# Attention, greedy MoE and Sinkhorn MoE in one kernel: GpSimd taken out of the routing rounds, and each expert's tokens turned inside the second layer of the expert ahead

## The chip, the cores and the metric

The kernel runs on one core of one Trainium2 chip. The metric is the device time of one execution in microseconds; the median of several runs counts. TensorE is called PE below, VectorE DVE, ScalarE ACT, GpSimd POOL; SP is the engine whose queue issues most DMAs.

## What is computed

Three stages follow each other, all in float32. Attention with a sink of 4 keys and a window of 128 over 2 x 8 heads, 768 positions, 64 dimensions gives 1536 tokens of 512 values. A first mixture of experts routes greedily: all 1536 x 8 logits are walked through from the highest down, a token goes to the first expert that still has room for it (192 tokens each), and only that expert's two layers run on it. A second mixture runs all 8 experts on every token and weighs them with a matrix P that eight Sinkhorn steps normalise by rows and columns.

```python
for idx in order:
    tok, e = (int(idx) // E, int(idx) % E)
    if assigned[tok] >= 0 or counts[e] >= cap:
        continue
    assigned[tok] = e
    counts[e] += 1
...
    h = np.maximum(x[mask] @ w1[e], 0.0)
    out[mask] = h @ w2[e]
...
    h = np.maximum(x @ w1[e], 0.0)
    ye = h @ w2[e]
    out += P[:, e:e + 1] * ye
```

## The kernel before

**Routing.** The greedy walk is done in eight rounds (`route`, L580). Each round fills one expert: every token proposes its best open expert, and `count` (L549) finds for each token how many proposals of the same expert stand ahead of it. For that, DVE builds for every chunk `c` of 128 tokens a 0/1 block `g` (which tokens have a higher logit, L566 and L568) and the block on the diagonal, `gt`, where equal logits count only if they come earlier. For odd chunks `gt` is one DVE operation (L561), for even ones two POOL operations (L564, L565). PE multiplies the blocks with the proposals into `cnt` (L574). There are twelve chunks in rounds 1 to 3, then `compact` (L493) squeezes the open tokens into six chunks for rounds 4 to 7; round 0 uses counts made during attention. From `cnt` DVE and PE find the expert that is full first, its tokens' slots as one-hot blocks `oh` (L623), their indices `ix` (L637), and `gather` (L658) has POOL issue two indirect DMAs that fetch the expert's 192 tokens into `xg` (two tiles, one buffer each). Weights of the expert come in four 1 MB DMAs on SP's queue (`load_w`, L647).

**First MoE.** `moe1(r)` (L689) turns the gathered tokens by eight PE transposes (L699) and two ACT copies (L701) into `xe` (one buffer), runs the first layer (L707, copied by ACT to `hT`, L709), then the second (L718, two halves of two blocks each, copied by ACT to `yT`, L720). `operands(r)` (L668) then splits results, and for experts 2, 3, 6 and 7 four sums `T1` to `T4` of results (DVE, L679 to L682), into a rounded part (ACT, L686) and a low part, the rest (L687: POOL, for the last expert DVE). The second MoE multiplies with these. Last come the logits of the second MoE (L727). All the PSUM tiles of the expert work are called `mm` and share three buffers. For expert 0 an edge (`issue_after`) keeps the transposes behind the third group of counts of round 1.

**Order.** The loop at L732 traces round `r` with high priority and then `moe1(r - 1)`; a planner at build time gives every engine one fixed order, routing first where it takes it to be ready, expert work in between. After the loop come the preparation of the first weights of the second MoE (`prepare`, L432: ACT rounds them, POOL makes sums `S` and the low parts, L447 to L452 and L464) and `moe1(7)`. On the chip each engine issues its own list in order.

**Second MoE.** `moe2` (L755) is a long pipeline of matmuls (L800, L857) over 32 chunks of weights, from about 430 us to the end.

Of the kernel before, what the change touches and what calls it, by code (L numbers as in the profile page):

```python
# [8 lines left out]
F32 = mybir.dt.float32  # L9
# [4 lines left out]
OP = mybir.AluOpType  # L14
# [6 lines left out]
def kernel(  # L21
# [16 lines left out]
    nc = tc.nc  # L38
    B, H, S, D = q.shape
    N, DM = out.shape  # L40
    E = moe_w_gate.shape[1]
    F = moe_w1.shape[2]
    P = 128
# [3 lines left out]
    CAP = N // E  # L47
# [15 lines left out]
    KD = DM // P  # L63
# [28 lines left out]
    before = rp.tile([P, P], F32, name="before")  # L92
# [3 lines left out]
    beforeb = rp.tile([P, P], BF, name="beforeb")  # L96
# [374 lines left out]
    def routing_and_moe1():  # L471
# [3 lines left out]
        mp = cx.enter_context(tc.tile_pool(name="mp", bufs=2))  # L475
# [10 lines left out]
        nc.gpsimd.tensor_copy(mv[:, :, 4 * E:], code)  # L486

        IDX = {}
        TP = 2
        st = dict(n=NCH, L=L, val=val, code=code, prop=prop0, m=m0)  # L490
        BIG = 2.0 ** 100

# [56 lines left out]
        def count(n, m, prop, row):  # L549

            cnt = ps.tile([P, n, E], F32, name="cnt", bufs=1)
            nc.tensor.matmul(cnt.rearrange("p c e -> p (c e)"), zb, zb[:, :n * E], start=True, stop=False,
                             skip_group_check=True)
            for c0 in range(0, n, GC):
                c1 = min(n, c0 + GC)
                blocks = []
                for c in range(c0, c1):
                    g = gp.tile([P, n, P], BF, name="g", bufs=GB)
                    gt = gp.tile([P, P], BF, name="gt", bufs=GB)
                    if c % TP:  # L560
                        nc.vector.scalar_tensor_tensor(gt, row[:, c], m[:, c:c + 1], before, op0=OP.is_equal,  # L561
                                                       op1=OP.mult)
                    else:
                        nc.gpsimd.tensor_scalar(gt, row[:, c], m[:, c:c + 1], None, op0=OP.is_equal)  # L564
                        nc.gpsimd.tensor_mul(gt, gt, beforeb)  # L565
                    nc.vector.tensor_scalar(g[:, :c + 1], row[:, :c + 1], m[:, c:c + 1], None, op0=OP.is_lt)  # L566
                    if c + 1 < n:
                        nc.vector.tensor_scalar(g[:, c + 1:], row[:, c + 1:], m[:, c:c + 1], None, op0=OP.is_le)  # L568
                    blocks += [(c, gt, prop[:, c, :])] + [(cc, g[:, cc, :], prop[:, c, :]) for cc in range(n)]

                first = None
                for cc, a, b in reversed(blocks):
                    with nullcontext() if first is None else tc.issue_after(first.ins):
                        mm = nc.tensor.matmul(cnt[:, cc, :], a, b, start=False, stop=(a is blocks[0][1] and c1 == n),  # L574
                                              skip_group_check=True)
                    first = first or mm
                st.setdefault("counted", []).append(mm.ins)
            return cnt
# [62 lines left out]
        W, XG, YT = {}, {}, {}  # L641
# [5 lines left out]
        def load_w(r, mats=(0, 1), q=nc.sync):  # L647
            e = q.value_load(EIX[0:1, r:r + 1], min_val=0, max_val=E - 1)
            for a in mats:
                src = (moe_w1, moe_w2)[a][bass.ds(e, 1)].rearrange("o (k p) f -> p (o k) f", p=P)  # L650
                for h in range(2):
                    t = bp.tile([P, WT], F32, name="wf", tag="w", bufs=WB)
                    t = t.rearrange("p (k f) -> p k f", f=DM if a else F // 2)
                    q.dma_start(t, src[:, h * KF // 2:(h + 1) * KF // 2] if a
                                else src[:, :, h * F // 2:(h + 1) * F // 2])
                    W.setdefault(r, ([], []))[a].append(t)
# [11 lines left out]
        def operands(r):  # L668
            t, h = divmod(r, 4)
            h, o = divmod(h, 2)  # L670
            K2_ = KD // 2
            block = lambda r: (YT[r // 2][:, a * K2_:(a + 1) * K2_, r % 2 * CAP:(r % 2 + 1) * CAP] for a in (0, 1))
            lo, hi = block(r)
            if h == 0:
                new = {"B11": lo, "B21": hi}
            else:
                lo0, hi0 = block(r - 2)
                T = {n: mp.tile([P, K2_, CAP], F32, name=n, bufs=1) for n in ("T1", "T2", "T3", "T4")}
                nc.vector.tensor_sub(T["T1"], lo, lo0)  # L679
                nc.vector.tensor_sub(T["T2"], hi, T["T1"])  # L680
                nc.vector.tensor_sub(T["T3"], hi, lo)
                nc.vector.tensor_sub(T["T4"], hi0, T["T2"])  # L682
                new = {"B22": hi, **T}
            for n, x in new.items():
                xh, xl = (y[:, :, o * CAP:(o + 1) * CAP] for y in XO[n][t])
                nc.scalar.activation(xh, x, AF.Copy)  # L686
                (nc.vector if r == E - 1 else nc.gpsimd).tensor_sub(xl, x, xh.bitcast(F32))  # L687

        def moe1(r):  # L689

            w1, w2 = W.pop(r)
            xg = XG.pop(r)
            xe = mp.tile([P, KD, CAP], F32, name="xe", bufs=1)
            with tc.issue_after(st["counted"][KC]) if r == 0 else nullcontext():
                for k0 in range(0, KD, 2):
                    pt = pm.tile([P, 2, CAP], F32, name="mm", tag="mm", bufs=3)
                    for k in (k0, k0 + 1):
                        for a in range(2):
                            nc.tensor.transpose(pt[:, k - k0, a * HC:(a + 1) * HC], xg[a][:HC, k * P:(k + 1) * P],  # L699
                                                ident[:HC, :HC])  # L700
                    nc.scalar.activation(xe[:, k0:k0 + 2, :], pt, AF.Copy)  # L701
            hT = mp.tile([P, KF, CAP], F32, name="hT", bufs=1)
            for j0 in range(0, KF, 2):
                ph = pm.tile([P, 2, CAP], F32, name="mm", tag="mm", bufs=3)
                for j in (j0, j0 + 1):
                    for k in range(KD):
                        nc.tensor.matmul(ph[:, j - j0, :], w1[j // JH][:, k, j % JH * P:(j % JH + 1) * P], xe[:, k, :],  # L707
                                         start=(k == 0), stop=(k == KD - 1))
                nc.scalar.activation(hT[:, j0:j0 + 2, :], ph, AF.Relu)  # L709
            if r % 2 == 0:  # L710
                YT[r // 2] = mp.tile([P, KD, 2 * CAP], F32, name="yT", bufs=2)
            yT = YT[r // 2]
            s0 = r % 2 * CAP
            for k0 in range(0, KD, 2):
                py = pm.tile([P, 2, CAP], F32, name="mm", tag="mm", bufs=3)
                for k in (k0, k0 + 1):
                    for j in range(KF):
                        nc.tensor.matmul(py[:, k - k0, :], w2[j // JH][:, j % JH, k * P:(k + 1) * P], hT[:, j, :],  # L718
                                         start=(j == 0), stop=(j == KF - 1))
                nc.scalar.activation(yT[:, k0:k0 + 2, s0:s0 + CAP], py, AF.Copy)  # L720
            operands(r)

            c0, c1 = s0 // P, (s0 + CAP) // P
            pl = ps.tile([P, 2, E], F32, name="lg", bufs=1)
            for a in range(c0, c1):
                for k in range(KD):
                    nc.tensor.matmul(pl[:, a - c0, :], yT[:, k, a * P:(a + 1) * P], wg2[:, k, :],  # L727
                                     start=(k == 0), stop=(k == KD - 1))
            c = r // 2 * (2 * CAP // P)
            nc.vector.tensor_copy(L2[:, c + c0:c + c1, :], pl[:, :c1 - c0, :])  # L730

        for r in range(E):  # L732
            with tc.high_priority(offset=HP):
                got = route(r)
                place_tokens(r, *got)
                if r + 1 == E // 2:
                    compact(NC2)
                if r + 1 < E:
                    propose()
                if r == 0:  # L740

                    with tc.issue_after(st["shown"]):
                        load_w(0, (1,), nc.scalar)
            if r == E - 1:
                rcx.close()
                pools.append(ctx.enter_context(tc.tile_pool(name="stg", bufs=1, side="right", reuse_waits="tile")))
            if r > 0:
                moe1(r - 1)
        run(prepare(*chunks[0]))
        moe1(E - 1)  # L750
        return cx

    def moe2(cx):  # L755
# [127 lines left out]
        for n in range(len(units) + 1):  # L883
# [7 lines left out]
            for _ in range(7):  # L891
# [4 lines left out]
                next(b, None)  # L896

    cx = routing_and_moe1()
    cx.close()
    moe2(ctx)  # L900
# [33 lines left out]
```

## Time and profile before

| what | value |
|---|---|
| median of 3 runs | 1449.2 us (1447.0 to 1450.65) |
| the profiled execution, its own time | 1455.11 us |
| its span, first to last instruction | 1453.0 us |
| its mean granted PE clock | 0.973 |
| PE busy | 1403.7 us, 97% of the span |
| DVE, ACT, POOL busy | 833.8, 461.8, 487.7 us |

The profile is one execution, recorded instruction by instruction. Busy times say how long an engine had something to do; what an engine waited for is put down to the instruction that released it. The granted clock of PE has two levels, 2.4 GHz (1.0) and 1.2 GHz (0.5); a value in between is the mean over a stretch.

### The profile page before, as it was taken

Reading aid. Unit: us, or ns where it says so; the run is one execution under the profiler, and the core shown is the slowest. Engines: PE = TensorE matmul, PEld = TensorE weight load, DVE = VectorE, ACT = ScalarE, POOL = GpSimd, SP = SyncE. Lnnn points to the kernel's source line nnn. Section 1 sums busy time; section 2 is a strip of 40 time slices with the busy share of each in tenths; the row PEclk is TensorE's granted clock in tenths of the full one; section 3 lists DMA queues with packets and bytes.
Section 4 is the critical chain, followed back from the end, with each engine's and each line's share of the span. In section 5 each row is a group of like instructions: output and inputs, shape, how many; then the busy total and the mean of one; then the engine's idle time right before and its main releaser. Section 6 shows DMA issues by size and latency. Waiting matters only on the chain.

```text
span 1453.0 us, 20938 instructions
## 1 busy us (share of the span) xinstructions
PE 1403.7 (97%) x8275; PEld 1241.0 (85%) x8275; DVE 833.8 (57%) x1822; ACT 461.8 (32%) x975; POOL 487.7 (34%) x472
## 2 busy tenths in 40 slices
PE   7999599999988999999999999999999999999998
PEld 4667499889987889888889889889888888888987
DVE  4667777771037565555555555555655555555554
ACT  4566111121233333223223223323323323323321
POOL 1136554351262223223433223433322432322303
PEclk9999599999998999999999999999999999999999
DMA  7331445657611000100100100100100100100002
GB/s 128 95 78 38 123 147 128 178 84 203 215 44 30 29 30 29 44 29 29 44 30 30 44 30 30 44 30 30 44 29 29 44 30 30 39 34 30 15 1 87
DMA packets 87338, 87.39 MB, mean 60 GB/s; under 512 B 43976, under 2 KB 60360, under 8 KB 87240
## 3 DMA queue, kind: packets, MB, share of 16 engines
q1 hardware_dynamic: 82696, 74.50, 17.9%
q0 software_dynamic: 2944, 9.44, 2.8%
q10 hardware_dynamic: 1600, 2.11, 0.4%
q8 instruction: 65, 1.06, 0.3%
q14 instruction: 33, 0.27, 0.1%
HBM read 79.75 MB, written 6.30 MB: 59 GB/s over the span
## 4 chain that ended last, share of the span: by engine, by line
PE 88%; DVE 7%; issue 1%; DMA 1%; ACT 1%; POOL 1%; SPq 0%; POOLq 0%; DVEq 0%; ACTq 0%
PE pa L857 36%; PE X L800 18%; PE Z L800 9%; PE mm L707 6%; PE Y L800 5%; PE mm L718 3%; PE S L241 2%; PE o L296 2%; PE PT L283 2%; DVE g L568 1%; PE ms L308 1%; DMA wf<-in_moe_w_dram 1%; DVE g L566 1%; PE tr L217 1%; PE cnt L574 1%
## 5 line engine op out<-in xcount | busy, mean ns | idle before, releaser
L857 PE MATMUL pa<-w,h 128*128 128x512 f32 x2304 | 597.2, 395 | 0.0
L857 PEld LDWEIGHTS pa<-w,h 128*128 128x128 f32 x2304 | 427.8, 188 | 67.8 <-ACT h L807 0.3
L868 DVE SCALAR_TENSOR_TENSOR accs<-pa,Pm,accs 128x512 f32<-128x512 f32 x360 | 269.1, 748 | 211.9 <-PE pa L857 211.9
L808 DVE SCALAR_TENSOR_TENSOR h<-sum,h 128x384 fp32r<-128x384 f32 x192 | 156.1, 813 | 99.1 <-ACT h L807 99.0
L447 POOL TENSOR_TENSOR w1l<-r,w1h 128x512 fp32r<-128x512 f32 x64 | 64.7, 1032 | 429.8 <-ACT w1h L446 416.3
L807 ACT ACTIVATE h<-sum 128x384 fp32r<-128x384 f32 x192 | 100.4, 523 | 207.9 <-DVE sum L817 207.9
L464 POOL TENSOR_TENSOR w<-r,w 128x1024 fp32r<-128x1024 f32 x32 | 77.0, 2407 | 235.6 <-ACT w L463 235.6
L812 ACT ACTIVATE u<-X 128x384 f32<-128x384 f32 x64 | 31.5, 492 | 268.6 <-PE X L800 268.6
L707 PE MATMUL mm<-xe,wf 128*128 128x192 f32 x512 | 104.6, 360 | 3.6 <-ACT xe L701 3.6
L707 PEld LDWEIGHTS mm<-xe,wf 128*128 128x128 f32 x512 | 92.3, 210 | 5.4 <-ACT xe L701 4.3
L718 PE MATMUL mm<-hT,wf 128*128 128x192 f32 x512 | 90.2, 329 | 0.0
L447 POOL TENSOR_TENSOR w1l<-S,w1h 128x1024 fp32r<-128x1024 f32 x32 | 86.9, 2714 | 0.0
L718 PEld LDWEIGHTS mm<-hT,wf 128*128 128x128 f32 x512 | 82.9, 190 | 0.0
L817 DVE TENSOR_TENSOR sum<-Z,u 128x384 f32<-128x384 f32 x64 | 35.7, 558 | 58.9 <-ACT u L812 58.9
L812 ACT ACTIVATE v<-X 128x384 f32<-128x384 f32 x64 | 31.4, 491 | 78.0 <-PE X L800 78.0
L254 ACT ACTIVATE pb<-pb,nb 128x264 f32<-128x264 f32 (+1 forms) x96 | 46.5, 488 | 14.4 <-DVE nb L249 13.2
L808 DVE SCALAR_TENSOR_TENSOR h<-X,h 128x384 fp32r<-128x384 f32 x64 | 35.7, 558 | 22.0 <-ACT h L807 22.0
L817 DVE TENSOR_TENSOR sum<-Z,v 128x384 f32<-128x384 f32 x64 | 35.7, 558 | 18.6 <-PE Z L800 18.5
L807 ACT ACTIVATE h<-X 128x384 fp32r<-128x384 f32 x64 | 31.5, 492 | 46.2 <-PE X L800 46.1
L446 ACT ACTIVATE w1h<-r 128x512 fp32r<-128x512 f32 x64 | 30.0, 516 | 48.5 <-PE Z L800 46.2
L244 DVE CUSTOM_DVE_ANT_0 pb<-S,M 128x264 f32<-128x264 f32 (+1 forms) x96 | 36.5, 403 | 13.9 <-PE S L241 13.1
L709 ACT ACTIVATE hT<-mm 128x384 f32<-128x384 f32 x32 | 15.7, 490 | 88.2 <-PE mm L707 83.8
(291 smaller groups left out, 2435.2 us busy)
## 6 DMA issues: line engine op xcount, KB each, us to landing
r<-in_moe_w_dram SPq DMA_DIRECT2D x64, 512.0 KB, 3.5
wf<-in_moe_w_dram SPq DMA_DIRECT2D x30, 1024.0 KB, 7.1
kn<-in_k_dram SPq DMA_DIRECT2D x12, 256.0 KB, 3.7
qn<-in_q_dram SPq DMA_DIRECT2D x12, 256.0 KB, 3.9
vn<-in_v_dram SPq DMA_DIRECT2D x12, 256.0 KB, 3.7
X<-xs POOLq DMA_DIRECT2D x12, 256.0 KB, 2.4
wf<-in_moe_w_dram ACTq DMA_DIRECT2D x2, 1024.0 KB, 11.4
xg<-X,ix POOLq DMA_INDIRECT x16, 8.7
```

The source lines that it names most:

```text
L254: nc.scalar.activation(PB[c][:, h, :w], PB[c][:, h, :w], AF.Exp, bias=NB[c][:, 0, h:h + 1], scale=scale, accum_out=NB[c][:, 2, h:h + 1])
L447: nc.gpsimd.tensor_sub(w1[1][:, o:o + n], x, w1[0][:, o:o + n].bitcast(F32))
L464: nc.gpsimd.tensor_sub(w2[:, 1], r2, w2[:, 0].bitcast(F32))
L707: nc.tensor.matmul(ph[:, j - j0, :], w1[j // JH][:, k, j % JH * P:(j % JH + 1) * P], xe[:, k, :], start=(k == 0), stop=(k == KD - 1))
L718: nc.tensor.matmul(py[:, k - k0, :], w2[j // JH][:, j % JH, k * P:(k + 1) * P], hT[:, j, :], start=(j == 0), stop=(j == KF - 1))
L800: nc.tensor.matmul(acc_, w1[a][:, o, k, :], XO[x][t][b][:, k, :], start=(start and n == 0), stop=(stop and n == 3 * KH - 1), skip_group_ch ...
L807: nc.scalar.activation(t[:, 0], x, AF.Relu)
L808: nc.vector.scalar_tensor_tensor(t[:, 1], x, 0.0, t[:, 0].bitcast(F32), op0=OP.max, op1=OP.subtract)
L812: nc.scalar.activation(t, x, AF.Copy)
L817: nc.vector.tensor_add(t, a, b)
L857: nc.tensor.matmul(pa, HT[u, f, h][:, a, j * P:(j + 1) * P], w2[:, b, f, :], start=(n == 0), stop=(n == 3 * FP - 1))
L868: nc.vector.scalar_tensor_tensor(acc[:, c], pa, pe, acc[:, c], op0=OP.mult, op1=OP.add)
```

## The change

Three edits. The diagonal blocks `gt` are all built by DVE, in one operation each; the two POOL operations for even chunks go. The low parts in `operands` are all subtracted by DVE. And the turning of the tokens becomes a function of its own, `turn_tokens(r)`: it is called within the second layer of expert `r - 1`, after the first half of that layer is copied to `yT`, and for expert 0 directly ahead of `moe1(0)`, where it stood before.

```diff
--- before.py
+++ after.py
@@ -486,7 +486,6 @@
         nc.gpsimd.tensor_copy(mv[:, :, 4 * E:], code)
 
         IDX = {}
-        TP = 2
         st = dict(n=NCH, L=L, val=val, code=code, prop=prop0, m=m0)
         BIG = 2.0 ** 100
 
@@ -557,12 +556,7 @@
                 for c in range(c0, c1):
                     g = gp.tile([P, n, P], BF, name="g", bufs=GB)
                     gt = gp.tile([P, P], BF, name="gt", bufs=GB)
-                    if c % TP:
-                        nc.vector.scalar_tensor_tensor(gt, row[:, c], m[:, c:c + 1], before, op0=OP.is_equal,
-                                                       op1=OP.mult)
-                    else:
-                        nc.gpsimd.tensor_scalar(gt, row[:, c], m[:, c:c + 1], None, op0=OP.is_equal)
-                        nc.gpsimd.tensor_mul(gt, gt, beforeb)
+                    nc.vector.scalar_tensor_tensor(gt, row[:, c], m[:, c:c + 1], before, op0=OP.is_equal, op1=OP.mult)
                     nc.vector.tensor_scalar(g[:, :c + 1], row[:, :c + 1], m[:, c:c + 1], None, op0=OP.is_lt)
                     if c + 1 < n:
                         nc.vector.tensor_scalar(g[:, c + 1:], row[:, c + 1:], m[:, c:c + 1], None, op0=OP.is_le)
@@ -684,13 +678,14 @@
             for n, x in new.items():
                 xh, xl = (y[:, :, o * CAP:(o + 1) * CAP] for y in XO[n][t])
                 nc.scalar.activation(xh, x, AF.Copy)
-                (nc.vector if r == E - 1 else nc.gpsimd).tensor_sub(xl, x, xh.bitcast(F32))
-
-        def moe1(r):
-
-            w1, w2 = W.pop(r)
+                nc.vector.tensor_sub(xl, x, xh.bitcast(F32))
+
+        XE = {}
+
+        def turn_tokens(r):
+
             xg = XG.pop(r)
-            xe = mp.tile([P, KD, CAP], F32, name="xe", bufs=1)
+            xe = XE[r] = mp.tile([P, KD, CAP], F32, name="xe", bufs=1)
             with tc.issue_after(st["counted"][KC]) if r == 0 else nullcontext():
                 for k0 in range(0, KD, 2):
                     pt = pm.tile([P, 2, CAP], F32, name="mm", tag="mm", bufs=3)
@@ -699,6 +694,12 @@
                             nc.tensor.transpose(pt[:, k - k0, a * HC:(a + 1) * HC], xg[a][:HC, k * P:(k + 1) * P],
                                                 ident[:HC, :HC])
                     nc.scalar.activation(xe[:, k0:k0 + 2, :], pt, AF.Copy)
+
+        def moe1(r):
+
+
+            w1, w2 = W.pop(r)
+            xe = XE.pop(r)
             hT = mp.tile([P, KF, CAP], F32, name="hT", bufs=1)
             for j0 in range(0, KF, 2):
                 ph = pm.tile([P, 2, CAP], F32, name="mm", tag="mm", bufs=3)
@@ -718,6 +719,8 @@
                         nc.tensor.matmul(py[:, k - k0, :], w2[j // JH][:, j % JH, k * P:(k + 1) * P], hT[:, j, :],
                                          start=(j == 0), stop=(j == KF - 1))
                 nc.scalar.activation(yT[:, k0:k0 + 2, s0:s0 + CAP], py, AF.Copy)
+                if k0 == 0 and r + 1 < E:
+                    turn_tokens(r + 1)
             operands(r)
 
             c0, c1 = s0 // P, (s0 + CAP) // P
@@ -744,6 +747,8 @@
             if r == E - 1:
                 rcx.close()
                 pools.append(ctx.enter_context(tc.tile_pool(name="stg", bufs=1, side="right", reuse_waits="tile")))
+            if r == 1:
+                turn_tokens(0)
             if r > 0:
                 moe1(r - 1)
         run(prepare(*chunks[0]))
```

## Rows read from the trace of the kernel before

**Rows 1.** The page: busy time of each engine, share of the span, instructions.
```profile
PE 1403.7 (97%) x8275; PEld 1241.0 (85%) x8275; DVE 833.8 (57%) x1822; ACT 461.8 (32%) x975; POOL 487.7 (34%) x472
```

**Rows 2.** Busy time by stretch; last three: granted PE clock, DMA share, GB/s.
```profile
190.00:340.00 150.00, 141.96 (x1336) 130.63 (x1333) 110.26 (x358) 30.05 (x61) 66.03 (x72) 0.94 0.58 147
480.00:1453.00 973.00, 966.70 (x4817) 867.93 (x4815) 558.26 (x816) 298.45 (x551) 306.19 (x241) 1.00 0.10 34
```

**Rows 3.** Timeline of PE: start, us, engine, line, tiles, [idle before <-releaser].
```profile
204.45 0.18 PE L574 MATMUL cnt<-prop,gt 128*128 128x8 bf16 x1 [0.65 <-POOL gt L565]
...
293.98 0.18 PE L574 MATMUL cnt<-prop,gt 128*128 128x8 bf16 x1 [1.82 <-POOL gt L565]
...
332.85 1.12 PE L628 MATMUL sm<-oh,codec 128*2 128x192 bf16 x6 [2.43 <-DVE oh L623]
...
405.30 12.19 PE L707 MATMUL mm<-xe,wf 128*128 128x192 f32 x56 [3.37 <-ACT xe L701]
```

**Rows 4.** Busy time by stretch, where the granted clock is low.
```profile
216.70:222.20 5.50, 5.49 (x40) 5.32 (x41) 1.12 (x4) 0.34 (x1) 0.70 (x1) 0.50 0.00 0
293.98:297.00 3.02, 3.02 (x13) 3.02 (x14) 2.51 (x6) 0.52 (x1) 1.86 (x2) 0.67 0.20 23
297.00:300.00 3.00, 3.00 (x17) 3.00 (x17) 1.90 (x14) 0.49 (x1) 1.00 (x1) 0.76 0.10 8
333.00:336.00 3.00, 3.00 (x14) 2.14 (x12) 0.35 (x1) 0.49 (x1) 0.00 (x0) 0.50 0.42 124
336.00:340.00 4.00, 4.00 (x16) 3.98 (x17) 0.16 (x1) 0.00 (x0) 0.00 (x0) 0.58 0.74 262
405.00:408.00 3.00, 2.70 (x8) 2.70 (x9) 0.00 (x0) 0.25 (x1) 3.00 (x4) 0.50 0.00 0
408.00:412.00 4.00, 4.00 (x17) 4.00 (x17) 0.00 (x0) 0.49 (x1) 2.76 (x4) 0.62 0.00 0
```

**Rows 5.** Groups by line, 160 to 428 us, and one DVE instruction of the timeline.
```profile
L564 POOL TENSOR_SCALAR gt<-row,m 128x128 bf16<-128x128 f32 x30 | 31.8, 1064 | 21.8 <-DVE ix L637 10.6 <-ACT row L546 8.4 <-PE cnt L574 2.5
L565 POOL TENSOR_TENSOR gt<-gt,beforeb 128x128 bf16<-128x128 bf16 x30 | 19.4, 653 | 1.6
...
L561 DVE SCALAR_TENSOR_TENSOR gt<-row,m,before 128x128 bf16<-128x128 f32 x30 | 12.3, 410 | 0.0
...
424.46 0.56 DVE L687 TENSOR_TENSOR xT1l<-T,xT1h 128x384 fp32r<-128x384 f32 x1 [0.59 <-ACT xT1h L686]
```

**Rows 6.** Timeline of DVE and POOL in round 7.
```profile
327.43 2.88 DVE L606 TENSOR_SCALAR eh<-iota_e,t 128x8 f32<-128x8 f32 x1
...
327.36 1.01 POOL L687 TENSOR_TENSOR xT2l<-T,xT2h 128x384 fp32r<-128x384 f32 x1
...
329.27 1.01 POOL L687 TENSOR_TENSOR xT4l<-T,xT4h 128x384 fp32r<-128x384 f32 x1
```

**Rows 7.** Timeline of POOL, DVE and ACT between the last two experts.
```profile
401.24 2.65 POOL L447 TENSOR_TENSOR w1l<-S,w1h 128x1024 fp32r<-128x1024 f32 x1
...
401.62 2.69 DVE L682 TENSOR_TENSOR T<-yT,T 128x384 f32<-128x384 f32 x1
...
404.34 0.52 ACT L686 ACTIVATE xT4h<-T 128x384 fp32r<-128x384 f32 x1 [2.09 <-DVE T L682]
404.77 0.47 ACT L701 ACTIVATE xe<-mm 128x384 f32<-128x384 f32 x1
```

**Rows 8.** POOL's gathers and ACT's copy, timeline; DMA issues: count, us to landing.
```profile
199.75 0.99 POOL L663 DMA_INDIRECT xg<-X,ix  x1 [13.06 <-DVE ix L637]
...
202.44 1.37 POOL L663 DMA_INDIRECT xg<-X,ix  x1 [0.17 <-issue]
...
207.13 0.49 ACT L720 ACTIVATE yT<-mm 128x384 f32<-128x384 f32 x1 [5.98 <-PE mm L718]
...
xg<-X,ix POOLq DMA_INDIRECT x16, 8.7
...
xg<-X,ix POOLq DMA_INDIRECT x1, 13.4
```

## The prediction

> **What bounds the kernel now.** I read the page first: TensorE (PE) is busy 1403.7 us of a span of 1453.0 [rows 1], so only what it waits, or runs at a lower clock, can be saved. The table by stage says where not to look: from 480 us to the end it is busy 966.7 of 973 us at full clock, and no edit is in that stage [rows 2]. From 190 to 340 us, where rounds of routing and the first MoE share the engines, it waits some 8 us and its granted clock is 0.94 [rows 2]. PE's timeline with the releasers of its waits gives the ones that bear on the change [rows 3]: 0.65 us at 204 for a `gt` of GpSimd (POOL), and a second just like it in the next round; 1.82 us at 294 for another; 2.43 us at 333 for a one-hot `oh` of VectorE (DVE); 3.37 us at 405 for the tokens `xe` of the last expert. The longer ones cost twice. Behind them the granted clock falls from 2.4 to 1.2 GHz: in the windows of [rows 4] the share lost is one minus the clock, so 3.0 us at 0.67 and 3.0 at 0.76 lose 1.0 + 0.7 = 1.7 us after the wait at 294; 1.5 + 1.7 = 3.2 after 333; 1.5 + 1.5 = 3.0 after 405. Behind the 0.65 us no fall is seen; I count none there.
>
> **Diagonals (L560 to L565).** Thirty pairs on POOL go, 31.8 + 19.4 us of its time [rows 5], and DVE gets thirty `gt` of the kind of L561, mean 0.41 us: 12.3 us over seven rounds, 2.5 in each of three rounds with twelve chunks, 1.2 in each of four with six. DVE gets something back: some of its time is waiting for POOL. The plainest case is in round 7: L606, an operation on 128x8, lasts 2.88 us, and it ends with the last of three subtractions of POOL that fill 327.4 to 330.3 [rows 6]. What POOL's diagonals hold in this way no row isolates. Bounds: nothing comes back (2.5 us a long round, 12.3 in all), or all that POOL did in the pairs (51.2 us [rows 5]) had stood in DVE's way, more than DVE gets. I take an even trade, near the lower end, because most `gt` of POOL are short beside a long `g`; then the rounds keep their length, and PE, which has expert work to fill in, sees nothing of it. What it does see is that the two waits of 0.65 and that of 1.82 on POOL go, since there is no `gt` left behind POOL's gathers: 3.1 us, and 1.7 of clock. **Gain 4.8.** What is late next is DVE's own `g`, on which PE already waits here and there.
>
> **Low parts (L687).** 23 subtractions for experts 0 to 6 go from POOL to DVE at 0.56 us each, the length of the one that DVE makes already [rows 5]: 12.9 us, two for each of experts 0, 1, 4 and 5, five for 2, 3 and 6. POOL's three at 327.4 were what held L606, and with it the chain to `oh`, on which PE waited 2.43 us. Without them the 2.88 us go; up to three subtractions, 1.7 us, may come between the links of the same chain, which leaves 2.88 - 1.7 = 1.2 and PE a wait of 2.43 - 1.2 = 1.2; at best the wait is gone. I keep 0.6 us of wait and let the clock stand: **gain** 2.43 - 0.6 + 3.2 = **5.0**, with 1.2 (half of the wait gone, the clock falling all the same) and 5.6 as ends. A low part waits for ACT's copy `xh`; behind it on DVE queue the next links of routing, which are due first in the planner's order, so I cost that at nothing while ACT is idle for most of the stage (30 of 150 us busy [rows 2]).
>
> **Turning the tokens ahead.** Eight transposes and two copies per expert move from behind the logits of the expert ahead into the middle of its second layer. The count of instructions stays; no DMA moves. For the last expert the gain is plain: its second copy to `xe` stood on ACT at 404.77, directly behind `xT4h`, which waited 2.09 us for the `T4` of DVE, which in turn lasted 2.69 beside a 2.65 us subtraction of POOL [rows 7]. Turned half a layer earlier, these copies come ahead of all of that: the wait of 3.37 and 3.0 us of clock go, **gain 6.4**. `T4` stays late, but nothing of PE waits for it in the next layer: the copies to `hT` come behind it on ACT, and three PSUM buffers cover them. If that cover were gone, the 2.09 us of ACT's wait would come back.
>
> Each gather into the single buffers `xg` is released earlier too, which is good for experts 5 to 7. For expert 1 it turns against the change. Its turn was due after expert 0; now it stands at the copy of the first half of `yT`, 207.13 before [rows 8], 206.5 without the wait at 204. Its second gather was issued at 202.44 behind a `gt`; without it, it follows the first one directly, 199.75 + 0.99, say 200.8 [rows 8]. Landing takes 8.7 us in the median of sixteen [rows 8], so 209.5: PE, which issues in order, would stand 3.0 us in the middle of the layer. Nothing in the trace shows this wait; its ends are none (the planner puts other work ahead) and the longest landing, 13.4 us [rows 8], that is 214.2 - 206.5 = 7.7 us. I take the median. For the clock I take 1.7, the loss behind the 1.82 us wait, between nothing behind 0.65 and 3.2 behind 2.43. **Loss 4.7.** The Trainium skill (SBUF — State Buffer, section "SBUF: two separate sides") warns of just this: descriptors of a DMA issued by GpSimd are held up while VectorE runs operations in a two-port mode. By that rule the 13.4 would be the figure to use, since DVE computes `g` without a break in that stretch, and the sum would lose 10.9 here, not 4.7; that landing is a rival below.
>
> **Sum.** 4.8 + 5.0 + 6.4 - 4.7 = 11.5 us off. The profiled execution took 1455.1 us by its own time, 5.9 above the median of the runs; I take the difference over to the median: 1449.2 - 11.5 = 1437.7.
>
> **Rivals.** (1) The gather lands late. For it: gathers run beside busy DVE, and one took 13.4. Against: expert 1's first one is of the ordinary kind. The stand is 7.7 us and the clock loses 3.2, 10.9 in place of 4.7: 1443.9. (2) DVE becomes the bound of the rounds, and the kernel gets slower. Nothing of POOL's absence comes back, each long round is 2.5 us longer by six `gt`, later ones also by low parts; expert 1's gather is issued 2.5 us later against a PE that isn't, so 3.0 + 2.5 + 3.2 = 8.7 us are lost at its turn, at most the same at expert 2's, and the wait for `oh` at 333 stays: 4.8 + 6.4 - 17.4, that is 6.2 slower, 1455.4. It decides once DVE gets back less than about half of what it is given. Against it speaks the 2.88 us L606 [rows 6]: what POOL does is felt on DVE. (3) The planner doesn't turn early: it holds the transposes back behind the rest of the layer. Then there is neither the gain of 6.4 nor the loss of 4.7: 9.8 off, 1439.4. (4) Better than the forecast: no stand at expert 1, the whole of 5.6 at 333, and the slow stretch from 216.7 to 222.2 at 0.50 [rows 4], 2.8 us lost behind a thin stretch of small matmuls that the transposes leave, goes as well: 4.8 + 5.6 + 6.4 + 2.8 = 19.6, 1429.6.
>
> **Chances.** Forecast 0.50, rival 1 0.17, rival 2 0.11, rival 3 0.13, rival 4 0.09. Runs of this kernel differ by a few us, so 0.3% (4.3 us) is about the least that a measurement tells from no change. Rival 2 is slower. Rival 1 lies at the edge of it, so a part of it counts as the same, with a part of the forecast's upper end: faster 0.79, same 0.11, slower 0.10. The range goes from rival 4 to just past rival 1, 1429 to 1445; it leaves out rival 2 and the tails.
>
> **What would show it.** Right: no wait of PE on POOL between 190 and 340 us; L606 of round 7 at the length of its neighbours; PE going from the last second layer but one into the last expert without a gap, its clock at 1.0 there; a wait of some 3 us at expert 1's turn, with the gather's landing at its end. Wrong: a longer DVE stretch from the first to the last `g` of a round (rival 2), transposes still behind the logits (rival 3), or a wait at expert 1 over 5 us (rival 1). Falls of the clock at new places would break the sum even with each step right.

## The result, and the profile after

| | kernel before | changed kernel |
|---|---|---|
| median, first measurement | 1449.93 us (4 runs) | 1434.58 us (1433.8 to 1440.94, 4 runs) |
| ratio, 95% interval | | 0.9904 (0.9882 to 0.9927) |
| the same kernel once more, last experiment below | 1449.95 us (11 runs) | 1436.12 us (6 runs), 0.9907 (0.9879 to 0.9935) |
| the profiled execution: own time, span | 1455.11, 1453.0 us | 1440.94, 1439.2 us |

So 14 to 15 us are gone; 11.5 were forecast, and 1434.6 to 1436.1 lies 2 to 3 us under the 1437.7, inside the range. The ratios, here and below, are as they were measured; they differ by up to 0.2% from the quotient of the medians beside them. In the page POOL lost 76 us of work, DVE got 5 more in total, PE is busy 9 us less with the same 8275 instructions [rows 1]:

```profile
PE 1394.8 (97%) x8275; PEld 1233.9 (86%) x8275; DVE 839.0 (58%) x1875; ACT 460.9 (32%) x975; POOL 412.0 (29%) x389
```

Where the time went is seen best from the end of attention to the first matmul of the Sinkhorn step, 438.84 us before and 425.39 after. The stretches by table, first the kernel before, then the changed one (columns as in [rows 2]):

```profile
160.00:438.00 278.00, 252.86 (x2118) 238.00 (x2117) 147.78 (x432) 59.31 (x118) 117.07 (x119) 0.91 0.55 145
```
```profile
160.00:424.60 264.60, 244.20 (x2118) 231.31 (x2117) 153.27 (x485) 58.48 (x118) 41.63 (x36) 0.94 0.57 152
190.00:340.00 150.00, 145.65 (x1405) 136.18 (x1403) 109.05 (x395) 30.87 (x63) 10.50 (x10) 0.97 0.56 148
340.00:415.00 75.00, 75.00 (x483) 74.62 (x483) 13.30 (x20) 21.29 (x44) 19.78 (x18) 1.00 0.60 172
```

Both traces are of executions 5 to 6 us above the median of their kernel, so they can be compared. PE has the same 2118 matmul records in both, in 13.4 us less. Of these, 4.7 are waits (278.00 - 252.86 = 25.1 before, 264.60 - 244.20 = 20.4 after), and 8.7 are busy time, because less of the same work ran at 1.2 GHz: the granted clock is 0.94 in place of 0.91. From 340 to 415 us, where the kernel before stood 3.37 us for the last expert's tokens, PE is never idle and its clock is 1.0. Not all is gain: from 318 to 322 us the clock of the changed kernel was 0.58, some 1.7 us lost, with PE busy all that time and no wait ahead of it.

The waits that [rows 3] list are all gone; there are new ones, on the gathers. PE's timeline after (columns as in [rows 3]; `mm<-ident,xg` is the turning of tokens: the first row is expert 0, the next two expert 1, the fourth expert 2; the last is the first matmul of the Sinkhorn step), and a row of the table by stretch:

```profile
181.00 1.38 PE L694 MATMUL mm<-ident,xg 96*128 96x96 f32 x7 [1.40 <-DMA xg<-X,ix]
...
208.00 0.30 PE L694 MATMUL mm<-ident,xg 96*128 96x96 f32 x1 [1.65 <-DMA xg<-X,ix]
210.14 1.22 PE L694 MATMUL mm<-ident,xg 96*128 96x96 f32 x6 [1.84 <-DMA xg<-X,ix]
...
245.09 0.80 PE L694 MATMUL mm<-ident,xg 96*128 96x96 f32 x7 [0.86 <-DMA xg<-X,ix]
...
425.39 0.48 PE L770 MATMUL gmx<-ident,gm 128*128 128x128 f32 x1 [3.73 <-DVE gm L768]
...
209.40:216.20 6.80, 6.06 (x46) 6.05 (x47) 2.73 (x6) 1.39 (x3) 0.00 (x0) 0.50 0.02 5
```

Expert 1's turn costs 1.65 + 1.84 = 3.5 us of waiting, and from 209.4 us, within the second wait, to 216.2 the clock is down (0.50): PE is busy for 6.06 us of that, so 3.0 are lost. DVE's operations of the rounds, by groups, 160 to 428 us, first before, then after (L600 is the former L606):

```profile
L566 DVE TENSOR_SCALAR g<-row,m 128x128 bf16<-128x128 f32 (+11 forms) x60 | 37.4, 633 | 2.8 <-ACT row L546 2.6
L568 DVE TENSOR_SCALAR g<-row,m 128x640 bf16<-128x640 f32 (+10 forms) x53 | 32.3, 618 | 0.1
L606 DVE TENSOR_SCALAR eh<-iota_e,t 128x8 f32<-128x8 f32 x8 | 5.2, 654 | 0.3
```
```profile
L560 DVE TENSOR_SCALAR g<-row,m 128x128 bf16<-128x128 f32 (+11 forms) x60 | 34.0, 566 | 0.0
L562 DVE TENSOR_SCALAR g<-row,m 128x640 bf16<-128x640 f32 (+10 forms) x53 | 28.2, 539 | 0.1
L559 DVE SCALAR_TENSOR_TENSOR gt<-row,m,before 128x128 bf16<-128x128 f32 x60 | 20.7, 344 | 10.2 <-PE cnt L568 7.6 <-ACT row L545 2.7
L600 DVE TENSOR_SCALAR eh<-iota_e,t 128x8 f32<-128x8 f32 x8 | 1.8, 230 | 0.2
```

Sixty `gt` cost 20.7 us where thirty cost 12.3 [rows 5], 8.4 more; the blocks `g` give back 3.4 + 4.1 = 7.5. That is the even trade.

### The profile page after: what moved, and what is told of

Its sections match the earlier page's. It is cut to its first block, busy times and chain, and to the rows that moved or that the text cites. A ratio compares the mean times of both kernels' runs of the same rounds, so it can differ in the third digit from the quotient of the medians.

```text
span 1439.2 us, 20856 instructions
## 1 busy us (share of the span) xinstructions
PE 1394.8 (97%) x8275; PEld 1233.9 (86%) x8275; DVE 839.0 (58%) x1875; ACT 460.9 (32%) x975; POOL 412.0 (29%) x389
## 4 chain that ended last, share of the span: by engine, by line
PE 91%; DVE 3%; DMA 2%; issue 2%; ACT 1%; POOL 0%; SPq 0%; POOLq 0%; DVEq 0%; ACTq 0%
PE pa L862 37%; PE X L805 18%; PE Z L805 9%; PE mm L719 5%; PE mm L708 5%; PE Y L805 5%; PE S L241 2%; DMA xg<-X,ix 2%; PE o L296 2%; PE PT L283 1%; PE ms L308 1%; PE cnt L568 1%; PE tr L217 1%; ACT pb L254 1%; PE lg L730 1%
## 5 line engine op out<-in xcount | busy, mean ns | idle before, releaser
L708 PE MATMUL mm<-xe,wf 128*128 128x192 f32 x512 | 96.6, 340 | 0.0
L719 PE MATMUL mm<-hT,wf 128*128 128x192 f32 x512 | 96.0, 337 | 0.0
L708 PEld LDWEIGHTS mm<-xe,wf 128*128 128x128 f32 x512 | 84.9, 195 | 0.9 <-issue 0.3
L657 POOL DMA_INDIRECT xg<-X,ix x16 | 16.3, 1020 | 192.6 <-DVE ix L631 126.7
```

## The experiments

**One part alone.** Three kernels each make one of the three edits to the kernel before; a fourth is the changed kernel with the low parts given back to POOL.

```diff
  e1_diag: the kernel before, and
-                    if c % TP: ... else: nc.gpsimd.tensor_scalar(gt, ...); nc.gpsimd.tensor_mul(gt, gt, beforeb)
+                    nc.vector.scalar_tensor_tensor(gt, row[:, c], m[:, c:c + 1], before, op0=OP.is_equal, op1=OP.mult)
  e2_low: the kernel before, and
-                (nc.vector if r == E - 1 else nc.gpsimd).tensor_sub(xl, x, xh.bitcast(F32))
+                nc.vector.tensor_sub(xl, x, xh.bitcast(F32))
  e3_turn: the kernel before, and turn_tokens as in the change
  e7_nolow: the changed kernel, and
-                nc.vector.tensor_sub(xl, x, xh.bitcast(F32))
+                (nc.vector if r == E - 1 else nc.gpsimd).tensor_sub(xl, x, xh.bitcast(F32))
```

> The kernel before with only the diagonals moved to DVE. Theory (each part has its own place): PE's waits on POOL (0.65, 0.65, 1.82 us) and the fall of the clock behind the last of them go, 4.8 us; L606 of round 7 still lasts about 2.9 us and PE still waits about 2.4 us for the one-hot blocks behind it and 3.4 us for the last expert's tokens. Time about 1445, the ratio 0.997. Rival (DVE becomes the bound): the stretch of g and gt in a long round grows from 17 us to over 19, and the time is at or above the kernel before.

> The kernel before with only the low parts moved to DVE. Theory: L606 of round 7 lasts 0.2 us and PE's wait for the one-hot blocks at the end of routing falls from 2.4 us to under 1.2, with no fall of the clock behind it; PE's waits on POOL's diagonals stay (the long one shorter by the one subtraction that stood in POOL's queue, so 0.8 to 1.8 us), the 3.4 us at the last expert stay. Time about 1445, ratio 0.997. Rival (the diagonals or the gathers of POOL held L606, not the subtractions): L606 still lasts over 1 us and the wait stays.

> The kernel before with only the tokens turned ahead. Theory: the wait of 3.4 us at the last expert and the fall of the clock behind it go (6.4 us); in their place PE waits for the gather of expert 1 in the middle of the second layer, 3 to 5 us, with a fall of the clock; the waits on POOL and the one for the one-hot blocks stay. Time about 1447 to 1450, ratio 0.999 to 1.000. Rival (the planner holds expert 1's transposes back when POOL issues its second gather later): no wait there and about 1443, ratio 0.996.

> The changed kernel with the low parts of experts 0 to 6 back on POOL. Theory: an operation of DVE's chain in the last rounds is held for 1 to 3 us by POOL's subtractions again, and PE waits for the one-hot blocks or another link of that chain; about 5 us slower than the changed kernel, 1440. Rival (with the gathers ahead and the diagonals gone POOL's subtractions fall beside other work): as the changed kernel, 1435.

| kernel | median us | ratio to the kernel before, interval |
|---|---|---|
| kernel before, beside these | 1452.42 (29 runs) | |
| diagonals alone | 1443.55 | 0.9945 (0.992 to 0.997) |
| low parts alone | 1449.72 | 0.9986 (0.9955 to 1.0018) |
| turning alone | 1448.34 | 0.9989 (0.9967 to 1.001) |
| all but the low parts | 1438.54 | 0.9934 (0.9909 to 0.9959) |

Of the three single edits only the diagonals are clear of no change: 0.55%, 8 us, where the working had 4.8 (0.33%, inside the interval). The other two by themselves are not told from none. The sum of the three, 0.55 + 0.14 + 0.11 = 0.80%, is near the 0.93 to 0.96% of all together. The low parts are worth 2.4 to 4 us on top of the other two (1438.54 against 1434.58 and 1436.12; the intervals overlap).

The trace with the diagonals alone shows why the two can't be added as I did. It is of the shortest of ten runs (1438.13 us), so it shows what meets what, not what the edit is worth. POOL still makes its subtractions there, but L606 (now L601) is not held any more, against what I had expected, and in place of the 2.43 us for `oh` in round 7 there are two smaller waits at other places, together longer. From its groups by line, its DVE timeline and its PE timeline:

```profile
L601 DVE TENSOR_SCALAR eh<-iota_e,t 128x8 f32<-128x8 f32 x8 | 1.8, 230 | 0.2
L587 DVE TENSOR_TENSOR sel<-sel,Lc 128x48 f32<-128x48 f32 x4 | 2.0, 505 | 0.0
...
318.32 2.39 DVE L560 SCALAR_TENSOR_TENSOR gt<-row,m,before 128x128 bf16<-128x128 f32 x1
...
286.01 0.66 PE L623 MATMUL sm<-oh,codec 128*2 128x192 bf16 x6 [1.73 <-DVE oh L618]
...
322.35 0.30 PE L569 MATMUL cnt<-prop,g 128*128 128x8 bf16 x6 [1.36 <-DVE g L563]
394.35 9.37 PE L702 MATMUL mm<-xe,wf 128*128 128x192 f32 x56 [3.66 <-ACT xe L696]
```

POOL's subtractions merely hit other operations of the same chain. A diagonal of DVE's, 0.34 us otherwise, lasts 2.39 us, beside three of them that end at 320.56, and PE's wait of 1.36 us follows. The four `sel` take 505 ns here. They were held in the kernel before too (521); they take 468 in the changed kernel with the low parts on POOL, and 207 in the changed kernel, where POOL makes neither. The groups and a PE row of these three, in that order:

```profile
L592 DVE TENSOR_TENSOR sel<-sel,Lc 128x48 f32<-128x48 f32 x4 | 2.1, 521 | 0.0
```
```profile
L586 DVE TENSOR_TENSOR sel<-sel,Lc 128x48 f32<-128x48 f32 x4 | 1.9, 468 | 0.0
...
288.75 0.66 PE L622 MATMUL sm<-oh,codec 128*2 128x192 bf16 x6 [1.32 <-DVE oh L617]
```
```profile
L586 DVE TENSOR_TENSOR sel<-sel,Lc 128x48 f32<-128x48 f32 x4 | 0.8, 207 | 0.0
```

The traces with one of the other parts alone say the same. With the low parts alone `sel` takes 207 ns and L606 0.23 us, as expected. But L606 takes 0.23 us with the turning alone too, where POOL makes all its diagonals and subtractions, and PE's wait of 2.43 us is in none of the three. The row of L606 with the turning alone (the first round lies outside the window):

```profile
L606 DVE TENSOR_SCALAR eh<-iota_e,t 128x8 f32<-128x8 f32 x7 | 1.6, 231 | 0.2
```

So any of the edits, by changing the order, undoes that one meeting; only moving the low parts keeps the chain free of them. The wait of 1.82 us at 294 is not the diagonals' alone either: in the kernel before a low part stood between the two operations of that diagonal in POOL's queue (the rows below). With the low parts alone that wait is 0.28 us, and the two of 0.65 us are the longest on a diagonal.

```profile
292.56 0.99 POOL L687 TENSOR_TENSOR xB22l<-yT,xB22h 128x384 fp32r<-128x384 f32 x1
293.51 0.42 POOL L565 TENSOR_TENSOR gt<-gt,beforeb 128x128 bf16<-128x128 bf16 x1
```

The last row of the trace with the diagonals alone shows more. PE waits 3.66 us for the last expert's tokens there, longer than the 3.37 of [rows 3], and the 56 matmuls behind it take 9.37 us, not 12.19: the clock did not fall. Nor did it with the low parts alone, where PE waits the same 3.37 us as before:

```profile
399.24 9.37 PE L707 MATMUL mm<-xe,wf 128*128 128x192 f32 x56 [3.37 <-ACT xe L701]
```

A fall of the clock behind one given wait is no fixed cost of that wait.

With the turning alone the wait at the last expert is gone and the one at expert 1 is larger than in the changed kernel. POOL has a diagonal between the two gathers there, which puts the second off by 1.4 us, and they land after 9.0 us, not 7.2:

```profile
210.82 1.38 PE L700 MATMUL mm<-ident,xg 96*128 96x96 f32 x7 [6.46 <-DMA xg<-X,ix]
```

That is more than the 3 to 5 us expected. By itself, then, turning ahead gives with one hand and takes with the other, and the time is as expected (1447 to 1450).

**Expert 1 turned late.** If the wait for its gather is a loss of its own, taking it away must show.

```diff
-                if k0 == 0 and r + 1 < E:
+                if k0 == 0 and r + 1 < E and r + 1 not in LATE:
                     turn_tokens(r + 1)
...
             if r > 0:
+                if r - 1 in LATE:
+                    turn_tokens(r - 1)
                 moe1(r - 1)
```

`LATE` is `(1,)` in the first kernel, `(1, 2)` in the second.

> The changed kernel, but expert 1's tokens are turned behind expert 0 as in the kernel before, all others ahead. Theory (PE's waits for expert 1's gather are a loss of their own, 1.65 + 1.84 us, with 3.4 us of clock behind them): both go, 5 to 7 us faster than the changed kernel, about 1428 to 1430, ratio 0.986. Rival (the thin stretch at the end of expert 0 pulls the clock down anyway, as it did in the kernel before at 216.5): only the wait goes, 1431 to 1432.

> The changed kernel, but experts 1 and 2 are turned behind the expert ahead. Theory: as with expert 1 alone, and the wait of 0.86 us at expert 2 goes too: 1427 to 1429. Rival (once expert 1 no longer stops PE, PE comes to expert 2 earlier against its gather, and turning it early costs more than 0.86 us): this kernel is 2 to 4 us faster than the one with expert 1 alone. Other rival: no difference between the two, under 1 us.

Expert 1 late: 1430.46 us (1429.38 to 1432.96), ratio 0.9855 (0.9824 to 0.9886). Its six runs all lie below all ten of the changed kernel (1433.8 to 1440.97, the repeat at the end included), so the 3.5 us wait and what hangs on it cost 4 to 6 us by the medians, some 7 by the ratios; 4.7 had been put down for it. The rival holds in part: in the trace both waits are gone, but the clock is still down from 215.0 to 218.5 us, behind a wait of 0.64 us for expert 1's `xe`. This kernel beats the kernel before and the changed one. Experts 1 and 2 late: 1433.75 us (1430.71 to 1435.0), 0.9876 (0.9845 to 0.9908), a miss: the wait of 0.86 us brought nothing when it went, and the kernel is if anything 3 us slower than with expert 1 alone. I don't know why; the intervals overlap, and its runs had a lower mean clock (median 0.980 against 0.984).

**What holds the gather.** From the issue at 201.21 and 202.44 to the landing it takes 7.2 us in the changed kernel (here and below the median of its two DMAs). POOL's timeline:

```profile
201.21 0.92 POOL L657 DMA_INDIRECT xg<-X,ix  x1 [29.83 <-DVE ix L631]
202.44 1.28 POOL L657 DMA_INDIRECT xg<-X,ix  x1 [0.30 <-issue]
```

Two kernels move weights in time: the second layer's 2 MB of expert 1 are traced behind its gather, or in round 2.

```diff
  e6_w2behind                                      e8_w2later
-            load_w(r, (0,) if r == 0 else (0, 1))
+            load_w(r, (0,) if r <= 1 else (0, 1))    + ahead of it: if r == 2: load_w(1, (1,))
...
             gather(r)
+            if r == 1:
+                load_w(r, (1,))
```

> The changed kernel, but the 2 MB of expert 1's second layer are loaded behind its gather instead of ahead of it. Theory (the gather shares the DMA engines with 4 MB of weights and that sets its landing): it lands about 2 us earlier after its issue, and PE's two waits for it, 3.5 us, fall to under 1.5; 2 to 5 us faster than the changed kernel. Rival (the descriptors come late because DVE is busy, some 4 us pass from the issue to the first packet whatever else moves): the waits stay within 0.7 us of 3.5, and the time within 1 us of the changed kernel.

> The changed kernel, but the 2 MB of expert 1's second layer are loaded in round 2, so that no weights move near expert 1's gather. Theory (what holds the gather is DVE: beside g on 128 partitions its descriptors come slowly, and packets last 1 us and more, whatever else moves): the gather crawls from its issue on, at under 60 GB/s for the whole chip's DMA, and PE's waits at expert 1's turn stay at 3 us or more. Rival (weights on the same DMA engines set its landing): no weights in the way, landing under 4 us from the issue, PE's waits under 1 us, time 3 to 5 us below the changed kernel.

Both came out slower than the changed kernel, the first against both of its expectations: 1443.48 us, 0.9962 (0.994 to 0.9983), and 1443.97 us, 0.9963 (0.9942 to 0.9985). The gather landed 15.0 and 13.2 us after its issue. The second edit did not do what it was meant to. SP issued the weights at 202.18, right behind the gather's first DMA, though they are traced in round 2: both kernels have 2 MB of weights ahead of the gather and 2 MB directly behind its issue. The second kernel's DMA issues from 200.3 to 203.6 us (count, KB each, us to landing), its PE timeline, and its table by stretch (last column GB/s, the one ahead of it the busy share of the DMA engines, which can exceed 1):

```profile
wf<-in_moe_w_dram SPq DMA_DIRECT2D x2, 1024.0 KB, 15.8
xg<-X,ix POOLq DMA_INDIRECT x2, 13.2
...
212.05 0.42 PE L696 MATMUL mm<-ident,xg 96*128 96x96 f32 x1 [5.66 <-DMA xg<-X,ix]
218.24 1.22 PE L696 MATMUL mm<-ident,xg 96*128 96x96 f32 x6 [5.77 <-DMA xg<-X,ix]
...
202.00:206.00 4.00, 4.00 (x48) 3.83 (x47) 3.95 (x9) 0.60 (x1) 1.45 (x2) 1.00 1.47 77
206.00:210.00 4.00, 0.39 (x3) 0.09 (x1) 3.13 (x7) 0.49 (x1) 0.00 (x0) 1.00 0.93 34
210.00:212.00 2.00, 0.00 (x0) 0.00 (x0) 0.00 (x0) 0.00 (x0) 0.00 (x0) 0.59 0.35 26
212.00:214.00 2.00, 0.42 (x1) 0.18 (x1) 0.00 (x0) 0.00 (x0) 0.00 (x0) 0.50 0.49 103
214.00:216.00 2.00, 0.00 (x0) 0.00 (x0) 0.00 (x0) 0.00 (x0) 0.00 (x0) 0.50 1.08 409
```

and the changed kernel's, where the weights issued ahead of the gather are still moving:

```profile
201.00:205.00 4.00, 4.00 (x46) 3.81 (x44) 3.95 (x9) 1.20 (x2) 2.20 (x2) 1.00 1.06 389
205.00:210.00 5.00, 1.65 (x18) 1.19 (x14) 4.09 (x10) 0.49 (x1) 0.00 (x0) 0.94 0.92 289
```

So weights ahead of the gather do not set its landing: with half of them it lands later. A kernel with no weights near the gather was not run. In the second kernel the DMA engines move 34 to 77 GB/s for eight us, the gather and the weights behind it crawling together, and only from 214 us on 409. In the changed kernel they have weights issued long before to move for the first four us, at 389 GB/s, and the gather is through soon after. DVE makes `g` for most of the crawl (3.95 of 4, then 3.13 of 4 us), which is for the theory that DVE holds the gather; but it stands still from 210 on, because PE in its wait consumes no blocks and their four buffers are full, and the rate is still 26 and 103 GB/s for four us more, which is not. Two more kernels look at DVE's side. One makes the `g` of round 2 in a two-input form; the other makes all diagonals of a round first.

```diff
  e10_tt, round 2 only
-                    nc.vector.tensor_scalar(g[:, :c + 1], row[:, :c + 1], m[:, c:c + 1], None, op0=OP.is_lt)
+                    nc.vector.tensor_tensor(g[:, :c + 1], row[:, :c + 1], mb(c + 1), op=OP.is_lt)
  e11_gtfirst
+            for c in range(n):
+                gt = gp.tile([P, P], BF, name="gt", bufs=NCH)
+                nc.vector.scalar_tensor_tensor(gt, row[:, c], m[:, c:c + 1], before, op0=OP.is_equal, op1=OP.mult)
+                gts.append(gt)
             for c0 in range(0, n, GC):
```

> The changed kernel, but the blocks g of round 2 alone are made with a two-input form (tensor_tensor against the broadcast column) in place of the one-input form with a scalar. Theory (the fast one-input form keeps POOL's descriptors from being written): DVE takes longer for each block, 1.6 us or more for a chunk in place of 1.0, yet expert 1's gather lands within 5 us of its issue and PE's waits at expert 1's turn fall under 1 us; waits for g in round 2 grow. Rival (descriptors are slow by themselves or through weights): the gather takes 7 us and more, PE's waits stay at 3 us or more. The time itself says little, 1433 to 1445.

> The changed kernel, but in each round DVE makes the diagonals of all chunks first (two-input operations, some 3 us for twelve) and only then the blocks g, the first of them right behind the gather's issue. Theory: the descriptors are written in these 3 us, expert 0's and expert 1's gathers land 2 us or more earlier, PE's waits for xg fall from 6 us to under 2.5; 2 to 6 us faster than the changed kernel, 1429 to 1432. Rival (the diagonals hold the descriptors as much as g does): waits for xg as in the changed kernel, and PE waits up to 2 us longer for the first g of round 1; time 1434 to 1437.

The two-input form doesn't help: 1455.98 us in its one run, the gather lands after 10.1 us, PE waits 2.60 and 7.39, and 6.31 more at expert 2's turn. POOL's second gather instruction for expert 1 itself took 5.43 us beside it (0.96 to 1.37 in the kernels before and after and with the diagonals first), timelines of POOL, DVE and PE:

```profile
203.00 5.43 POOL L664 DMA_INDIRECT xg<-X,ix  x1 [0.30 <-issue]
...
203.35 4.28 DVE L564 TENSOR_TENSOR g<-row,m 128x1408 bf16<-128x1408 f32 x3
...
216.42 1.06 PE L701 MATMUL mm<-ident,xg 96*128 96x96 f32 x5 [7.39 <-DMA xg<-X,ix]
```

The Trainium skill (SBUF — State Buffer, section "Who interferes with whom") says that a VectorE instruction with two SBUF inputs contends with a GpSimd instruction that reads SBUF. The gather reads its indices there, and the 5.43 us agree. They don't single that form out: with the diagonals first, expert 4's second gather instruction took 6.03 us, and for 3.9 of them DVE made `g` in the one-input form (timeline of POOL):

```profile
290.01 6.03 POOL L661 DMA_INDIRECT xg<-X,ix  x1 [0.30 <-issue]
```

With the diagonals first, PE's waits on gathers fall from 6.1 us to 3.4, as hoped for, but its wait for the first `g` of round 1 grows from 2.56 to 4.28 us; 1433.62 us (1430.94 to 1437.26), 0.9896 (0.9867 to 0.9926), not told from the changed kernel. What makes a gather crawl, and the weights behind it with it, stays open.

**POOL kept away from DVE at another place.** The 3.7 us for `gm` are in both kernels. In the changed one DVE's last sums and low parts lie beside POOL's preparation of the second MoE (timeline of DVE; `T4` and two low parts left out):

```profile
415.56 2.74 DVE L675 TENSOR_TENSOR T<-yT 128x384 f32<-128x384 f32 x1
...
421.27 1.08 DVE L681 TENSOR_TENSOR xT3l<-T,xT3h 128x384 fp32r<-128x384 f32 x1
422.27 2.69 DVE L681 TENSOR_TENSOR xT4l<-T,xT4h 128x384 fp32r<-128x384 f32 x1
```

The kernel with expert 1 late was given an edge that keeps POOL back until the last low part is made:

```diff
+        held = lambda: tc.issue_after(HELD[0]) if (e, i) in ((0, 1), (0, 2)) else nullcontext()
...
+            with held():
                 nc.gpsimd.tensor_sub(w1[1][:, o:o + n], x, w1[0][:, o:o + n].bitcast(F32))
...
     cx = routing_and_moe1()
     cx.close()
+    last = consts.tile([P, 1], F32, name="last")
+    HELD.append(nc.gpsimd.tensor_copy(last, XO["T4"][1][1][:, 0, 2 * CAP - 1:2 * CAP].bitcast(F32)).ins)
```

> The changed kernel with expert 1 turned late, and POOL's preparation of the second and third chunk of the second MoE held behind the last low part of expert 7 (a one-column copy on POOL that reads it, and an order edge). Theory (a POOL subtraction holds DVE's two-input and fast operations for its whole length): without POOL beside them DVE's last sums and low parts take 0.5 us each and none takes 2.7, PE's wait of 3.7 us for the Sinkhorn maximum falls under 1 us: 4 to 7 us faster than with expert 1 late alone, 1423 to 1427. Rival (that wait comes from ACT's copies or from DVE's own sum of work): DVE's operations stay at 1.0 us, the wait stays over 2.5 us, 1430.

```profile
409.20 0.55 DVE L681 TENSOR_TENSOR T<-yT 128x384 f32<-128x384 f32 x1
...
411.07 0.55 DVE L687 TENSOR_TENSOR xT3l<-T,xT3h 128x384 fp32r<-128x384 f32 x1
411.54 0.56 DVE L687 TENSOR_TENSOR xT4l<-T,xT4h 128x384 fp32r<-128x384 f32 x1
...
417.92 0.50 PE L871 MATMUL pa<-w,h 128*128 128x512 f32 x1 [1.77 <-ACT h L821]
...
423.84 0.74 PE L814 MATMUL Z<-xB22h,w1h 128*128 128x384 f32 x2 [2.28 <-DVE sum L831]
```

The mechanism is as expected to the instruction: 0.55 us each, where it was 1.08 to 2.74, and the wait for `gm` is gone. The time is not: 1431.73 us (1429.72 to 1435.12), 0.9888 (0.986 to 0.9916), no better than without the edge. POOL makes the same subtractions some us later, now beside the first operations of the second MoE, and PE has new waits of 1.77 and 2.28 us for these. The stall moved on.

**The changed kernel again.**

> The changed kernel itself once more, unaltered, as the measure for the runs that alter one thing in it. If its four runs so far are typical: ratio to the kernel before 0.990, median 1434 to 1436, PE's waits for expert 1's gather 3.5 us in its trace, and the kernel with expert 1 turned late stays below it by 3 us or more. Rival (that difference is scatter of the clock between executions): a median at or under 1432, or scatter over the range of the kernel with expert 1 late.

1436.12 us (1434.89 to 1440.97), 0.9907; its waits for expert 1's gather are 1.98 + 1.43 us, and its clock does not fall at 318 us. The difference to the kernel with expert 1 late stands. Single runs differ with the granted clock: 17 runs of the kernel before, taken beside the kernel with expert 1 late, go from 1445.73 us at 0.982 to 1460.06 at 0.970.

## Why the prediction was right

- **The bound.** PE and its waits were the right place to look: the stage from 470 us on is as before, and the gain is all ahead of it.
- **Diagonals (4.8).** The waits on POOL went, and the even trade on DVE was measured as one (8.4 against 7.5 us). By its median the term was undersized, 8 us alone, with 4.8 just inside the interval. What it missed is the fixed order: with the diagonals moved, L606 no longer meets POOL's subtractions, so a part of what I had booked under the low parts came with the diagonals. It comes with the turning as well, and of the 1.82 us that I gave to the diagonals a low part made up 0.99. What the rest of the 8 us is, the one trace of that kernel doesn't show.
- **Low parts (5.0).** Mechanism right, size off: 2 us by themselves, not told from none, and 2.4 to 4 on top of the rest, under the 5.0 I took though above the lower end of 1.2. The 2.88 us of L606 were one meeting of POOL's subtractions with one instruction, in one fixed order; the lasting part is that POOL holds something of that chain in each order in which it makes the low parts (521, 505 and 468 ns for `sel`, against 207 in the two kernels where DVE makes them).
- **Turning ahead (6.4 - 4.7).** Both came: no wait at the last expert, and a wait of 3.5 us at expert 1, forecast as 3.0. That the 3.0 came so near is luck: the second gather was issued at 202.44, not at 200.8, since the first came 1.5 us later than before, and it landed after 7.7 us, not 8.7. The price in time, 4 to 7 us, is near the 4.7. The clock was down for 6.8 us, 3.0 lost, where I took 1.7. The edit alone gives 1.6 us, the working 1.7, but the interval goes from 4.8 us gained to 1.5 lost and decides nothing.
- **The clock.** I charged each fall to the wait ahead of it, 7.9 us in all, 6.2 with the 1.7 at expert 1 taken off. Summed over the stage the busy time fell by 8.7 us, but the pairing failed: the wait at the last expert cost 3.0 us of clock in the trace before and none with the diagonals or the low parts alone, and from 318 to 322 us the changed kernel lost 1.7 with no wait. All three falls that I booked, behind 294, 333 and 405 us, are in the trace before and in none of the three with one part alone. So they were taken from one execution, 5.9 us above the median, and then subtracted from the median. What speaks for a gain by the clock all the same are the single runs: their mean clock has a median of 0.977 to 0.978 in the kernel before and of 0.982 in the changed one.
- **Rival 1**, the late landing, did not come: in the change as made the gather took 7.2 us, not 13.4. DVE was at work on `g` beside it for 3.95 of 4 and 4.09 of 5 us. The Trainium skill's warning (SBUF — State Buffer, section "SBUF: two separate sides"), that VectorE's two-port operations hold up the descriptors of a GpSimd DMA, was rightly given as a rival; these 7.2 us don't bear it out. With half of the weights behind the gather 13.2 and 15.0 us were seen, so such landings do occur, but whether DVE's work causes them no run shows.
- Rival 2, DVE as the new bound, is refuted by `g`; rival 3, the planner holding the transposes back, by the timeline.

The sum came out 2 to 3 us short, by terms that were off in both directions; that it came so near is in part luck.

## What to carry to other kernels

An engine that gets in the way of another's chain is worth emptying even if its own work is off the path: here small operations of POOL held links of DVE's chain, up to 2.9 us at a time, and PE waited for the end of that chain. Size such an edit by all the operations it can meet, not by the one meeting seen in a trace, since the next order of instructions has another. And when a step is moved ahead, check it for each pass of the loop: seven of the eight experts' turns wait no longer for their gather in the changed kernel than 1.8 us (expert 0's, which was not moved) or 0.9 us, and one, whose gather had not landed, waits 3.5; leaving that one where it was gave the lowest median, 1430.5 us.

## What the runs showed that I had not expected

- A gather landed in 7.2 us with 4 MB of weights issued ahead of it, and in 13.2 and 15.0 with 2 MB ahead and 2 MB directly behind. The weights behind it crawled along: its two DMAs of 1 MB took 15.8 us in the median, and from 206 to 210 us all engines together moved 34 GB/s at a busy share of 0.93.
- POOL's gather instruction, around 1 us as a rule, took 5.43 us beside two-input operations of DVE and 6.03 us beside mostly one-input ones.
- A wait of 3.66 us was followed by no fall of PE's clock, one of 3.37 us by a fall in one trace and by none in another, and one fall came with PE busy all the time.
